# A retention, Fourier and two-layer MLP kernel: Strassen-like products summed in PSUM, normalisation moved to ScalarE, and one block's first tiles made directly

## The chip, the cores and the metric

The kernel runs on one core of one Trainium2 chip. The metric is the device time of one execution in microseconds (us); each run also has a profile of one execution, whose span is the time from the first to the last recorded instruction. Engines are named as the profile names them: PE (TensorE matmuls), PEld (its weight loads), DVE (VectorE), ACT (ScalarE), POOL (GpSimd), SP (SyncE, which issues the transfers).

## What is computed

Two sequences of 768 tokens and 512 features go through a decaying attention (8 heads of 64), a Fourier mixing over tokens and features, and then two MLP layers with a residual each. Only the MLP layers are touched by the change:

```python
def _moe_ref(x, w_ch1, w_ch2):
    X = np.fft.fft(np.fft.fft(x, axis=1), axis=2)
    u = x + np.real(X)
    un = (u - mean(u)) / np.sqrt(var(u) + 1e-06)
    return u + np.maximum(un @ w_ch1, 0.0) @ w_ch2          # 512 -> 2048 -> 512
def _moe2_ref(x, g_ln, w_ch1, w_ch2):
    xn = (x - mean(x)) / np.sqrt(var(x) + 1e-06) * g_ln
    return x + np.maximum(xn @ w_ch1, 0.0) @ w_ch2
```

The weights come as 64-bit floats. They are converted on the chip, and every operand of a matmul is a pair of float16 tensors, a high part and a low rest, so that one product is three passes (high x high, high x low, low x high).

## The kernel before, in words

**Blocks and steps.** The 1536 tokens are four blocks of 384. A layer has 16 hidden tiles of 128 features for each block, so there are 2 x 4 x 16 = 128 steps; layer one takes the blocks as 0, 1, 2, 3, layer two as 0, 1, 3, 2. Step n makes a hidden tile ("up": `mlp_up`, or `mlp_up_fast` for a pair of tiles) and applies the one of three steps earlier ("down": `mlp_down`, 9 matmuls of 512 columns into the banks `ps_y`). Everything else is put at a step number by `put` and is issued between the up and the down of that step: attention of the second sequence, weight conversion (`w_conv`), layer normalisation (`ln_tasks`), and the sums that the fast form needs. From there a scheduler that keeps the order of a priority list, but lets ready work pass, decides the order on each engine; it was not written out by hand after the first 75 us. Names carry layer, block and tile: `h1_0_7` is layer two, block 0, tile 7.

**The two forms of the up step.** The direct form (`mlp_up`, L685) is 12 matmuls of 384 columns into one PSUM bank, then ReLU on ACT (L698) and the rest on DVE (L699). The fast form (L755) makes two tiles at once from 2x2 sub-blocks in Winograd's way: seven products of six matmuls of 192 columns in place of eight. It needs sums of the weights (`w1_sums`, tiles `ws` then `sw`, four of `[128, 2, 256]` for each group g of four tiles and each kk) and sums of the normalised tokens (`un_sums`, tiles `tr`, `ts`, then `th`). The even call makes four products in two banks (`ps_1`, `ps_2`), the odd call three in two others (`ps_3`, `ps_4`). ACT and DVE put them together in SBUF (tiles `sa`, `sb`; L790 to L809), and ReLU and rest read SBUF (L779, L780). Layer two uses the fast form throughout, layer one in block 3 and from tile 4 of block 2: 46 pairs.

**The weights of layer two.** The rooms of the first weight (`w1t`) and second weight (`w2t`) are shared by the layers, so the weights of layer two can be converted only as the last block of layer one frees the rooms. `w1_unit` (16 of them, from step 52 on, one every 1.5 steps) converts a quarter of a group and after every second one calls `w1_sums` with the float32 values still at hand; the 16 of `w2` come every second step from 51.5. A conversion is three DVE operations of 512 columns (L269, L271, L273), two on ACT (L283, L284) and one on POOL (L286). In layer two the first of the four weight sums is DVE's (L722), three are POOL's (L723 to L725), and the low parts are POOL's too (L729).

**Normalisation.** `ln_a` takes mean and variance, `ln_n` (L646) subtracts and scales a row tile of 512 columns on DVE, `ln_b` splits it (ACT, POOL) and sends it through a transposing transfer.

## Time and profile before

| | before |
|---|---|
| median of 3 runs | 652.61 us (651.95 to 653.06) |
| the profiled execution | 651.21 us, of which the span is 649.0 us |
| PE, PEld busy | 585.6 us (90%), 381.1 us (59%) |
| DVE, ACT, POOL busy | 511.0 us (79%), 257.3 us (40%), 315.9 us (49%) |
| mean granted clock of TensorE | 0.972 of full speed |
| work on the chain that ended last | PE 49%, DVE 33%, issue 8% |

How to read it: shares of busy time are means over stages with different limits, so the stages are looked at one by one. Durations overlap: the next matmul starts before the one ahead is recorded as ended, and the same holds a little for DVE. The cost of a repeated matmul is therefore taken from start to start.

### The profile page before, as it was taken

The numbers are of one execution on the slowest core, as the hardware profiler recorded it, in microseconds if no ns is written. First come the engines' busy times: TensorE is split into PE (matmuls) and PEld (weight loads), VectorE is DVE, ScalarE is ACT, GpSimd is POOL, SyncE is SP. The second block draws the span as 40 slices with busy tenths as digits, with TensorE's granted clock in tenths as the row PEclk, the third lists the DMA queues.
The fourth block names the chain that finished last, engine by engine and source line by source line (L and its number), as shares of the span: only waits on it lengthen the run. The fifth ranks groups of instructions, "written<-read, shape, count | busy, mean of one in ns | idle before, by whom it ended". The sixth has DMA issues, their size and how long they took to land.

```text
span 649.0 us, 12273 instructions
## 1 busy us (share of the span) xinstructions
PE 585.6 (90%) x4733; PEld 381.1 (59%) x4733; DVE 511.0 (79%) x1040; ACT 257.3 (40%) x523; POOL 315.9 (49%) x318
## 2 busy tenths in 40 slices
PE   6958968789999999789999877987999999999997
PEld 4733734445554455466767545754676777777673
DVE  6999897999898749976599999997974754565442
ACT  3645356875532422332245553654422312221120
POOL 7865668998755564731138774787311200120000
PEclk9979899999999999999999996998999999999999
DMA  9992019885200010011044433453020014201001
GB/s 264 352 395 75 7 60 243 229 287 167 67 2 1 1 33 18 0 38 14 1 113 150 145 115 105 140 161 115 1 66 18 17 50 54 45 2 65 34 1 49
DMA packets 47141, 59.98 MB, mean 92 GB/s; under 512 B 26095, under 2 KB 31084, under 8 KB 47084
## 3 DMA queue, kind: packets, MB, share of 16 engines
q1 hardware_dynamic: 46412, 59.13, 31.2%
q8 instruction: 37, 0.61, 0.4%
q14 instruction: 20, 0.16, 0.1%
q10 hardware_dynamic: 672, 0.08, 0.1%
HBM read 50.55 MB, written 4.72 MB: 85 GB/s over the span
## 4 chain that ended last, share of the span: by engine, by line
PE 49%; DVE 33%; issue 8%; POOL 3%; ACT 3%; DMA 3%; SPq 0%; DVEq 0%; ACTq 0%; POOLq 0%
PE ps_y L820 21%; PE ps L774 17%; DVE wf L273 4%; PE ps_h L692 3%; DVE ps_w L271 3%; DVE ps_w L269 3%; DMA ws<-in_w 2%; DVE wr L717 2%; DVE h L780 2%; DVE tr L737 2%; PE ps_s L329 1%; DVE bst L627 1%; DVE h L699 1%; DVE ws L722 1%; DVE u L828 1%
## 5 line engine op out<-in xcount | busy, mean ns | idle before, releaser
L820 PE MATMUL ps_y<-w,h 128*128 128x512 f16 x1152 | 274.0, 379 | 10.5 <-DVE h L780 3.7
L820 PEld LDWEIGHTS <-h 128*128 128x128 f16 x1152 | 109.2, 98 | 119.1 <-issue 6.4
L774 PEld LDWEIGHTS <-sw 128*128 128x128 f16 x1104 | 96.8, 100 | 27.2 <-issue 9.3
L286 POOL TENSOR_TENSOR w<-wf,w 128x512 f16<-128x512 f32 x64 | 77.1, 1209 | 59.6 <-ACT w L284 59.6
L774 PE MATMUL ps<-th,sw 128*128 128x192 f16 x828 | 96.4, 252 | 7.2 <-ACT th L749 4.3
L774 PEld LDWEIGHTS <-w 128*128 128x128 f16 x828 | 72.8, 99 | 19.0 <-issue 4.9
L692 PE MATMUL ps_h<-unT,w 128*128 128x384 f16 x396 | 73.0, 326 | 10.2 <-DVE h L699 4.7
L774 PE MATMUL ps<-unT,w 128*128 128x192 f16 x552 | 63.9, 251 | 3.2 <-DVE sb L791 1.1
L692 PEld LDWEIGHTS <-w 128*128 128x128 f16 x396 | 37.3, 98 | 39.8 <-ACT w L284 6.7
L655 POOL TENSOR_TENSOR uns<-un,uns 128x512 f16<-128x512 f32 x21 | 25.3, 1206 | 70.3 <-ACT uns L654 63.8
L780 DVE SCALAR_TENSOR_TENSOR h<-sb,h 128x384 f16<-128x384 f32 x46 | 31.4, 683 | 33.7 <-ACT h L779 33.7
L750 POOL TENSOR_TENSOR th<-ts,th 128x384 f16<-128x384 f32 x28 | 27.1, 984 | 59.5 <-ACT th L749 59.5
L779 ACT ACTIVATE h<-sa 128x384 f16<-128x384 f32 x46 | 23.9, 520 | 78.3 <-DVE sa L802 75.7
L779 ACT ACTIVATE h<-sb 128x384 f16<-128x384 f32 x46 | 24.0, 521 | 70.8 <-PE ps_y L820 55.3
L729 POOL TENSOR_TENSOR sw<-ws,sw 128x512 f16<-128x512 f32 x32 | 40.7, 1281 | 20.2 <-ACT sw L728 19.9
L283 ACT ACTIVATE wf<-wf 128x512 f32<-128x512 f32 x48 | 30.0, 628 | 34.5 <-DVE wf L273 34.2
L802 DVE TENSOR_TENSOR sa<-ps,sb 128x192 f32<-128x192 f32 x46 | 16.2, 351 | 30.5 <-PE ps L774 30.2
L269 DVE TENSOR_SCALAR ps_w<-ws 128x512 int32<-128x512 int32 x54 | 36.7, 683 | 3.8 <-DMA ws<-in_w 3.7
L284 ACT CAST w<-wf 128x512 f16<-128x512 f32 x64 | 38.6, 612 | 0.8
L808 DVE TENSOR_TENSOR sb<-ps,sb 128x384 f32<-128x384 f32 x46 | 25.4, 553 | 16.7 <-PE ps L774 16.2
L271 DVE SCALAR_TENSOR_TENSOR ps_w<-ws,ps_w 128x512 int32<-128x512 int32 x54 | 36.7, 684 | 0.2
L273 DVE SCALAR_TENSOR_TENSOR wf<-ws,ps_w 128x512 int32<-128x512 int32 x54 | 36.2, 676 | 0.3
(163 smaller groups left out, 938.4 us busy)
## 6 DMA issues: line engine op xcount, KB each, us to landing
ws<-in_w SPq DMA_DIRECT2D x25, 512.0 KB, 5.8
ws<-in_w2b SPq DMA_DIRECT2D x16, 512.0 KB, 3.3
ws<-in_w1b SPq DMA_DIRECT2D x16, 512.0 KB, 3.9
kt<-in_kt SPq DMA_DIRECT2D x12, 256.0 KB, 5.0
v<-in_v SPq DMA_DIRECT2D x12, 256.0 KB, 3.9
k<-in_k SPq DMA_DIRECT2D x12, 256.0 KB, 4.4
...
```

The costliest lines, as they stand in the source:

```text
L269: dve.tensor_scalar(part, raw[:, :, 1], 3, REST, op0=ALU.logical_shift_left, op1=ALU.bitwise_and)
L271: dve.scalar_tensor_tensor(part, raw[:, :, 1], KEEP, part, op0=ALU.bitwise_and, op1=ALU.bitwise_or)
L273: dve.scalar_tensor_tensor(ti, raw[:, :, 0], 29, part, op0=ALU.logical_shift_right, op1=ALU.bitwise_or)
L283: act.activation(t, t, AF.Copy, scale=sc)
L284: act.copy(hi, t)
L286: (dve if m == 0 and i in (LD1 if kind == 1 else LD2) else pool).tensor_tensor(lo, t, hi, op=ALU.subtract)
L692: pe.matmul(ps, w[:, i, k, fo:fo + P], x[:, j, k, :], start=n == 0, stop=n == 11)
L729: pool.tensor_tensor(lo, z, hi, op=ALU.subtract)
L774: pe.matmul(ps, lhs, rhs, start=n == 0, stop=n == 5)
L779: act.activation(h[:, 0], s, AF.Relu)
L780: dve.scalar_tensor_tensor(h[:, 1], s, 0.0, h[:, 0], op0=ALU.max, op1=ALU.subtract)
L820: pe.matmul(dn[blk][j], h[:, x, j * P:(j + 1) * P], w[:, y], start=f == 0 and n == 0, stop=f == NF - 1 and n == 2)
```

## The change

**What it does.** (1) The fast form keeps its sums in PSUM. A pair has two banks, `left` and `right`, one for each half of the 384 tokens. Products that are only added to one another are accumulated by the matmuls themselves (`start` only on the first write of a bank), and DVE adds the rest in place, in PSUM. The last two products are issued as `rest()` after the step's down. ReLU and rest read PSUM, and the hidden tiles of a pair share one buffer (`h_pair`, three buffers as before, each twice as large). (2) `ln_n` becomes one tiny DVE operation and an ACT operation of 512 columns with a scale and a bias per row. (3) Block 0 of layer two makes tiles 0 to 7 directly (`F1 = 8`); its token sums come eight steps later, and the weight sums of groups 0 and 1 are made from the converted weights at steps 72 to 78 in place of 53 to 63, with two more DVE additions of 512 columns each time (L728 in the changed code, the L717 of before).

```diff
+F1 = 8
@@ ln_n
-        dve.tensor_scalar(un, u, mv[:, 0:1], rs[:, 1:2], op0=ALU.subtract, op1=ALU.mult)
+        dve.scalar_tensor_tensor(rs[:, 0:1], mv[:, 0:1], -1.0, rs[:, 1:2], op0=ALU.mult, op1=ALU.mult)
+        act.activation(un, u, AF.Identity, bias=rs[:, 0:1], scale=rs[:, 1:2])
@@ mlp_act
+            pairs[key] = up_sb.tile([P, 2, 2, TB], F16, tag="h", name=f"h{m}_{blk}_{f // 2}")
...
-        h = up_sb.tile([P, 2, TB], F16, tag="h", name=f"h{m}_{blk}_{f}")
+        h = h_pair(m, blk, f)[:, f % 2]
@@ mlp_up_fast
-                    pe.matmul(ps, lhs, rhs, start=n == 0, stop=n == 5)
+                    pe.matmul(ps, lhs, rhs, start=start and n == 0, stop=n == 5, skip_group_check=True)
...
+            left = bank("up", f"ps_1{m}_{blk}_{f}")
+            right = bank("at", f"ps_2{m}_{blk}_{f}")
+            prod(left[:, :HB], "11", "11", start=True)
+            prod(left[:, HB:TB], 2, 2)
+            prod(right[:, :HB], 1, 1, start=True)
+            act.copy(m1, left[:, :HB])
+            dve.tensor_tensor(u2, left[:, HB:TB], m1, op=ALU.add)
...
+        prod(left[:, HB:TB], 3, 3)
+        prod(left[:, :HB], "12", "21")
+        dve.tensor_tensor(u3, left[:, HB:TB], m1, op=ALU.add)
+        dve.tensor_tensor(right[:, HB:TB], right[:, :HB], u3, op=ALU.add)
+        def rest():
+            prod(left[:, HB:TB], "22", 4)
+            prod(right[:, :HB], 4, "22")
+            dve.tensor_tensor(left[:, HB:TB], left[:, HB:TB], m1, op=ALU.add)
+            dve.tensor_tensor(right[:, :HB], right[:, :HB], u2, op=ALU.add)
+            h = h_pair(m, blk, f)
+            for x, ps in enumerate((left, right)):
+                hi, lo = (h[:, :, y, x * HB:x * HB + HB] for y in range(2))
+                z = ps[:, :TB].rearrange("p (f t) -> p f t", f=2)
+                act.activation(hi, z, AF.Relu)
+                dve.scalar_tensor_tensor(lo, z, 0.0, hi, op0=ALU.max, op1=ALU.subtract)
@@ w1_unit
-        else:
+        elif 4 * g >= F1:
             w1_sums(1, g, kk, (first.pop((g, kk)), t))
@@ the plan
-    fast_from.update({(1, blk): 0 for blk in range(NB)})
+    fast_from.update({(1, blk): F1 if i == 0 else 0 for i, blk in enumerate(order[1])})
-                put(at - TL + 2 * kk, lambda m=m, blk=blk, kk=kk: un_sums(m, blk, kk))
+                put(at + f - TL + 2 * kk, lambda m=m, blk=blk, kk=kk: un_sums(m, blk, kk))
+    for g in range(F1 // 4):
+        for kk in range(2):
+            put(n0 + NF + F1 + 2 * (2 * g + kk), later(lambda g=g, kk=kk: w1_sums(1, g, kk), PR1))
...
+        if rest:
+            rest()
```

**How it moves the instructions.** The first place is DVE in the last block (layer two, block 2). Before, a pair has eight DVE operations, and all but the reads of `ps_` are on SBUF:

```order
L791 TENSOR_TENSOR sb1_2_12_7984<-ps_11_2_12_7985,sa1_2_12_7983 128x192
L795 TENSOR_TENSOR sb1_2_12_7984<-ps_21_2_12_8000,sb1_2_12_7984 128x192
L796 TENSOR_TENSOR sa1_2_12_7983<-ps_21_2_12_8000,sa1_2_12_7983 128x192
L802 TENSOR_TENSOR sa1_2_12_7983<-ps_31_2_13_8024,sb1_2_12_7984 128x192
L808 TENSOR_TENSOR sb1_2_12_7984<-ps_41_2_13_8035,sb1_2_12_7984 128x384
L780 SCALAR_TENSOR_TENSOR h1_2_12_8032<-sa1_2_12_7983,h1_2_12_8032 128x384
L809 TENSOR_TENSOR sb1_2_12_7984<-ps_41_2_13_8035,sb1_2_12_7984 128x192
L780 SCALAR_TENSOR_TENSOR h1_2_13_8050<-sb1_2_12_7984,h1_2_13_8050 128x384
```

Of the change, one period of the same engine in the same block (`ps_1` is now the left bank, `ps_2` the right one; L798 makes `u2`, L805 `u3`):

```order
L805 TENSOR_TENSOR t1_2_13_7769<-ps_11_2_12_7726,s1_2_12_7725 128x192
L806 TENSOR_TENSOR ps_21_2_12_7727<-ps_21_2_12_7727,t1_2_13_7769 128x192
L798 TENSOR_TENSOR s1_2_14_7800<-ps_11_2_14_7801,s1_2_14_7800 128x192
L811 TENSOR_TENSOR ps_11_2_12_7726<-ps_11_2_12_7726,s1_2_12_7725 128x192
L812 TENSOR_TENSOR ps_21_2_12_7727<-ps_21_2_12_7727,s1_2_12_7725 128x192
L818 SCALAR_TENSOR_TENSOR h1_2_6_7795<-ps_11_2_12_7726,h1_2_6_7795 128x2x192
L818 SCALAR_TENSOR_TENSOR h1_2_6_7795<-ps_21_2_12_7727,h1_2_6_7795 128x2x192
```

Seven operations stand where eight stood; the one of 384 columns on `sb` is gone, and the first sum of the next pair (tile 14) now stands between the sums of this one.

The second place is POOL at the end of block 0 and the start of block 1 of layer two. `sw` are low parts of weight sums, `th` of token sums; the second block's first products read `th0_1_1_0` to `th1_1_1_1`. Before:

```order
L729 TENSOR_TENSOR sw1_3_1_5746<-ws12_1_3_1_5747,sw1_3_1_5746 128x512
L286 TENSOR_TENSOR w2_1_13_5915<-wf2_1_13_5910,w2_1_13_5915 128x512
L729 TENSOR_TENSOR sw1_3_1_5746<-ws34_1_3_1_5748,sw1_3_1_5746 128x512
L750 TENSOR_TENSOR th0_1_1_0_5902<-ts12_1_1_0_5896,th0_1_1_0_5902 128x384
L750 TENSOR_TENSOR th1_1_1_0_5905<-ts34_1_1_0_5897,th1_1_1_0_5905 128x384
L750 TENSOR_TENSOR th0_1_1_1_6008<-ts12_1_1_1_6002,th0_1_1_1_6008 128x384
```

Of the change, the end of the same stretch of POOL's order:

```order
L740 TENSOR_TENSOR sw1_1_0_5646<-ws12_1_1_0_5651,sw1_1_0_5646 128x512
L740 TENSOR_TENSOR sw1_1_0_5646<-ws34_1_1_0_5652,sw1_1_0_5646 128x512
L761 TENSOR_TENSOR th0_1_1_0_5695<-ts12_1_1_0_5689,th0_1_1_0_5695 128x384
L761 TENSOR_TENSOR th1_1_1_0_5698<-ts34_1_1_0_5690,th1_1_1_0_5698 128x384
L735 TENSOR_TENSOR ws34_1_1_1_5770<-wr1_1_1_5765 128x256
L734 TENSOR_TENSOR ws12_1_1_1_5769<-ws12_1_1_1_5769,wr1_1_1_5765 128x256
L736 TENSOR_TENSOR ws34_1_1_1_5770<-wr1_1_3_5766,ws12_1_1_1_5769 128x256
L740 TENSOR_TENSOR sw1_1_1_0_5763<-ws12_1_1_1_5769,sw1_1_1_0_5763 128x512
L740 TENSOR_TENSOR sw1_1_1_1_5764<-ws34_1_1_1_5770,sw1_1_1_1_5764 128x512
L288 TENSOR_TENSOR w2_1_15_5912<-wf2_1_15_5907,w2_1_15_5912 128x512
L761 TENSOR_TENSOR th0_1_1_1_5813<-ts12_1_1_1_5807,th0_1_1_1_5813 128x384
```

The weight sums of groups 0 and 1 of layer two, which POOL made in the last block of layer one, now stand among those of group 3 and ahead of the token sums of block 1.

The third place is DVE at tile 7 of the same block 0, the last direct tile (`h1_0_3` is the buffer of tiles 6 and 7). Before:

```order
L780 SCALAR_TENSOR_TENSOR h1_0_7_5538<-sb1_0_6_5461,h1_0_7_5538 128x384
L269 TENSOR_SCALAR ps_w1_1_13_5670<-ws1_1_13_5667 128x512
L722 TENSOR_TENSOR ws12_1_3_0_5571<-wf1_1_12_5494,wf1_1_14_5561 128x256
L271 SCALAR_TENSOR_TENSOR ps_w1_1_13_5670<-ws1_1_13_5667,ps_w1_1_13_5670 128x512
L791 TENSOR_TENSOR sb1_0_8_5591<-ps_11_0_8_5592,sa1_0_8_5590 128x192
L646 TENSOR_SCALAR un1_1_1_5622<-u0_105,mv1_1_1_5543,rs1_1_1_5545 128x512
```

Of the change:

```order
L710 SCALAR_TENSOR_TENSOR h1_0_3_5264<-ps_h1_0_7_5287,h1_0_3_5264 128x384
L756 TENSOR_TENSOR ts34_1_0_1_5314<-tr1_0_3_5311,ts12_1_0_1_5313 128x192
L733 TENSOR_TENSOR ws12_1_3_0_5348<-wf1_1_12_5269,wf1_1_14_5338 128x256
L275 SCALAR_TENSOR_TENSOR wf2_1_11_5449<-ws2_1_11_5447,ps_w2_1_11_5450 128x512
L271 TENSOR_SCALAR ps_w1_1_15_5534<-ws1_1_15_5531 128x512
L798 TENSOR_TENSOR s1_0_8_5367<-ps_11_0_8_5368,s1_0_8_5367 128x192
L273 SCALAR_TENSOR_TENSOR ps_w1_1_15_5534<-ws1_1_15_5531,ps_w1_1_15_5534 128x512
L635 TENSOR_SCALAR rs1_3_1_6173<-mv1_3_1_6171 128x1
L728 TENSOR_TENSOR wr1_0_0_5399<-w1_1_0_4361 128x512
L728 TENSOR_TENSOR wr1_0_2_5400<-w1_1_0_4361 128x512
```

The first weight sum of group 3 (`ws12_1_3_0`) stands behind the rest of tile 7 in both, and the added sums of group 0 (`wr1_0_0`, `wr1_0_2`) follow it.

## Rows read from the trace of the kernel before

**Rows 1.** Busy time by stage; MLP steps from 267 us on.
```profile
core 0: us, PE busy (x) PEld busy (x) DVE busy (x) ACT busy (x) POOL busy (x), PEclk, DMA share, GB/s
182.00:267.00 85.00, 80.30 (x517) 41.35 (x516) 69.41 (x139) 26.32 (x61) 48.35 (x48) 1.00 0.05 10
...
329.00:395.00 66.00, 56.09 (x422) 37.17 (x420) 65.18 (x127) 35.37 (x67) 46.54 (x45) 0.97 0.45 135
395.00:476.00 81.00, 72.60 (x547) 50.67 (x547) 75.43 (x159) 38.50 (x77) 49.25 (x48) 0.92 0.34 101
476.00:636.00 160.00, 160.00 (x1304) 113.50 (x1303) 86.73 (x218) 36.36 (x79) 15.60 (x17) 1.00 0.16 35
```

**Rows 2.** DVE in order of time where three blocks end: start, length, instruction.
```profile
328.16 0.68 DVE L828 SCALAR_TENSOR_TENSOR u<-ps_y,u 128x512 f32<-128x512 f32 x1
...
393.99 0.68 DVE L828 SCALAR_TENSOR_TENSOR u<-ps_y,u 128x512 f32<-128x512 f32 x1
...
473.96 1.88 DVE L831 SCALAR_TENSOR_TENSOR o<-ps_y,u 128x512 f32<-128x512 f32 x3
```

**Rows 3.** PE in order of time, one pair of tiles in layer two.
```profile
502.57 0.66 PE L774 MATMUL ps<-unT,sw 128*128 128x192 f16 x6
...
504.06 2.10 PE L820 MATMUL ps_y<-w,h 128*128 128x512 f16 x9
506.00 0.66 PE L774 MATMUL ps<-unT,w 128*128 128x192 f16 x6
...
507.98 1.24 PE L820 MATMUL ps_y<-w,h 128*128 128x512 f16 x5
```

**Rows 4.** The chain that ended last: one direct tile (start, length).
```profile
163.28 1.95 PE ps_h L692 x12
```

**Rows 5.** What PE waited for, 329 to 476 us: total, times, longest.
```profile
PE ps L774 <- ACT th L749: 4.3, 3, 3.0
PE ps_y L820 <- DVE h L780: 3.7, 5, 1.3
```

**Rows 6.** Groups of DVE, 329 to 476 us: busy us, mean ns of one | idle before.
```profile
L780 DVE SCALAR_TENSOR_TENSOR h<-sb,h 128x384 f16<-128x384 f32 x16 | 14.1, 882 | 0.9 <-ACT h L779 0.9
L780 DVE SCALAR_TENSOR_TENSOR h<-sa,h 128x384 f16<-128x384 f32 x17 | 13.0, 763 | 0.0
L808 DVE TENSOR_TENSOR sb<-ps,sb 128x384 f32<-128x384 f32 x16 | 8.8, 547 | 0.2
...
L802 DVE TENSOR_TENSOR sa<-ps,sb 128x192 f32<-128x192 f32 x17 | 5.9, 345 | 0.0
...
L646 DVE TENSOR_SCALAR un<-u,mv,rs 128x512 f32<-128x512 f32 x6 | 4.6, 760 | 0.0
...
L633 DVE TENSOR_SCALAR rs<-mv 128x1 f32<-128x1 f32 x6 | 0.9, 146 | 0.0
```

**Rows 7.** Groups of the whole run, shapes apart.
```profile
L283 ACT ACTIVATE wf<-wf 128x512 f32<-128x512 f32 x48 | 30.0, 628 | 34.5 <-DVE wf L273 34.2
...
L699 DVE SCALAR_TENSOR_TENSOR h<-ps_h,h 128x384 f16<-128x384 f32 x36 | 19.6, 548 | 5.7 <-ACT h L698 5.6
...
L717 DVE TENSOR_TENSOR wr<-w 128x512 f32<-128x512 f16 x16 | 14.2, 923 | 0.0
...
L283 ACT ACTIVATE wf<-wf,gsc 128x512 f32<-128x512 f32 x16 | 11.5, 721 | 8.7 <-DVE wf L273 8.6
```

**Rows 8.** Groups of POOL, 329 to 476 us.
```profile
L286 POOL TENSOR_TENSOR w<-wf,w 128x512 f16<-128x512 f32 x32 | 38.4, 1201 | 47.2 <-ACT w L284 47.2
L729 POOL TENSOR_TENSOR sw<-ws,sw 128x512 f16<-128x512 f32 x16 | 19.1, 1196 | 0.8 <-ACT sw L728 0.5
L750 POOL TENSOR_TENSOR th<-ts,th 128x384 f16<-128x384 f32 x8 | 8.3, 1046 | 10.8 <-ACT th L749 10.8
...
L723 POOL TENSOR_TENSOR ws<-ws,wf 128x256 f32<-128x256 f32 x8 | 7.1, 881 | 1.1 <-PE ps L774 0.4 <-DMA ws<-in_w2b 0.4 <-DVE ws L722 0.4
```

**Rows 9.** PE and ACT in order of time, last pair of layer two.
```profile
631.45 0.66 PE L774 MATMUL ps<-th,sw 128*128 128x192 f16 x6
...
632.14 0.32 ACT L790 COPY sa<-ps 128x192 f32<-128x192 f32 x1 [0.42 <-PE ps L774]
```

More of the change, by code (lines that the diff above doesn't have):

```diff
@@ L694, in mlp_up, with h_pair @@
         mlp_act(m, blk, f, ps)
+    pairs = {}
+    def h_pair(m, blk, f):
+        key = m, blk, f // 2
+        if key not in pairs:
+            pairs[key] = up_sb.tile([P, 2, 2, TB], F16, tag="h", name=f"h{m}_{blk}_{f // 2}")
+        return pairs[key]
     def mlp_act(m, blk, f, ps):
-        h = up_sb.tile([P, 2, TB], F16, tag="h", name=f"h{m}_{blk}_{f}")
+        h = h_pair(m, blk, f)[:, f % 2]
         act.activation(h[:, 0], ps, AF.Relu)
@@ L757, in mlp_up_fast, with prod @@
         w, x = w1t[m, g], unT[m, blk]
-        def prod(ps, wa, xb):
+        def prod(ps, wa, xb, start=False):
             n = 0
@@ L783, in mlp_up_fast @@
-        if f % 2 == 0:
-            s = {y: f32t(f"s{y}{m}_{blk}_{f}")[:, :TB] for y in "ab"}
-            fast[m, blk] = s
-            (a1, a2), (b1, b2) = ((s[y][:, :HB], s[y][:, HB:]) for y in "ab")
-            ps = bank("up", f"ps_1{m}_{blk}_{f}")
-            prod(ps[:, :HB], "11", "11")
-            prod(ps[:, HB:TB], 2, 2)
-            act.copy(a1, ps[:, :HB])
-            dve.tensor_tensor(b1, ps[:, HB:TB], a1, op=ALU.add)
-            ps = bank("at", f"ps_2{m}_{blk}_{f}")
-            prod(ps[:, :HB], "12", "21")
-            prod(ps[:, HB:TB], 1, 1)
-            dve.tensor_tensor(b2, ps[:, HB:TB], b1, op=ALU.add)
-            dve.tensor_tensor(a1, ps[:, :HB], a1, op=ALU.add)
-            return
@@ L798, in mlp_up_fast @@
-        s = fast.pop((m, blk))
-        (a1, a2), (b1, b2) = ((s[y][:, :HB], s[y][:, HB:]) for y in "ab")
-        ps = bank("up", f"ps_3{m}_{blk}_{f}")
-        prod(ps[:, :HB], 4, "22")
-        dve.tensor_tensor(a2, ps[:, :HB], b2, op=ALU.add)
-        finish(s["a"], f - 1)
-        ps = bank("at", f"ps_4{m}_{blk}_{f}")
-        prod(ps[:, :HB], 3, 3)
-        prod(ps[:, HB:TB], "22", 4)
-        both = s["b"].rearrange("p (x t) -> p x t", x=2)
-        dve.tensor_tensor(both, ps[:, :HB].unsqueeze(1).to_broadcast([P, 2, HB]), both, op=ALU.add)
@@ L809, in mlp_up_fast @@
-        dve.tensor_tensor(b1, ps[:, HB:TB], b1, op=ALU.add)
-        finish(s["b"], f)
+        if f % 2 == 0:
+            s = f32t(f"s{m}_{blk}_{f}")
+            m1, u2 = s[:, :HB], s[:, HB:TB]
+            left = bank("up", f"ps_1{m}_{blk}_{f}")
+            right = bank("at", f"ps_2{m}_{blk}_{f}")
+            fast[m, blk] = left, right, s
+            prod(left[:, :HB], "11", "11", start=True)
[3 more added lines that the diff above has]
+            dve.tensor_tensor(u2, left[:, HB:TB], m1, op=ALU.add)
+            return None
@@ new lines, in mlp_up_fast @@
+        left, right, s = fast.pop((m, blk))
+        m1, u2 = s[:, :HB], s[:, HB:TB]
+        prod(left[:, HB:TB], 3, 3)
+        prod(left[:, :HB], "12", "21")
+        u3 = f32t(f"t{m}_{blk}_{f}")[:, :HB]
+        dve.tensor_tensor(u3, left[:, HB:TB], m1, op=ALU.add)
[11 more added lines that the diff above has]
+                dve.scalar_tensor_tensor(lo, z, 0.0, hi, op0=ALU.max, op1=ALU.subtract)
+            for y in range(2):
+                hts[m, blk, f - 1 + y] = h[:, y]
@@ L812, in tile_retention_fourier_mlp @@
+        return rest
     dn = {}
@@ L1040, in tile_retention_fourier_mlp @@
     for n in range(total + LAG):
+        rest = None
         if n < total:
@@ L1043, in tile_retention_fourier_mlp @@
             if n >= SPL:
-                (mlp_up if f < fast_from.get((m, blk), NF) else mlp_up_fast)(m, blk, f)
+                rest = (mlp_up if f < fast_from.get((m, blk), NF) else mlp_up_fast)(m, blk, f)
         for _, _, task in sorted(bg.pop(n, ()), key=lambda z: z[0]):
```

5 lines of the change are left out of this document (removed).

## The prediction, made before the changed kernel was run

> **What bounds the kernel now.** I read the busy time by stage first, then the order of time on VectorE at the ends of blocks and on TensorE inside a pair, then what TensorE waited for, then the groups of VectorE, ScalarE and GpSimd.
>
> The stages are the first thing to see [rows 1]. From 476 us on TensorE is busy all the time at full clock: nothing that only relieves another engine can help there. A pair of tiles with its two downs takes 7.35 us there, worked out from [rows 3]: 18 matmuls of 512 columns in two lots of 9 at 1.94 us each (506.00 less 504.06; 216 ns each), and 42 matmuls of 192 columns in 1.49 us (504.06 less 502.57) plus 1.98 us (507.98 less 506.00), which is 3.47 us or 82.6 ns each. So a block of eight pairs costs 58.8 us of TensorE.
>
> The two blocks before that stage are another matter. Their ends, by the last residual addition of each, are 328.8, 394.7 and 475.8 us [rows 2], so they take 65.9 and 81.2 us, 147.0 together, where TensorE needs 2 x 58.8 = 117.6. Of the 29.4 us lost, TensorE is idle for 9.9 and 8.4 (66.0 less 56.09, 81.0 less 72.60), and the rest is mostly half clock: a granted 0.97 and 0.92 of the full 2.4 GHz is 0.03 x 66 + 0.08 x 81 = 8.5 us. VectorE is busy for 65.18 of 66.0 us and 75.43 of 81.0 [rows 1]. It is the bound of these two blocks; TensorE waits for `th` and for the rests `h` [rows 5], which stand in VectorE's and ScalarE's queues.
>
> **The change, part by part.**
>
> *The fast form, VectorE.* Before, a pair is five additions of 192 columns at 0.345, one of 384 at 0.547, and rests of 0.763 and 0.882 [rows 6]: 3.92 us. After, it is five additions of 192 and two rests that read PSUM. Such rests are not in these blocks, but the direct form has them, 384 columns from PSUM in 0.548 [rows 7]. With in-place additions at the same 0.345 the pair is 2.83 us. Nothing here shows an addition with both source and target in PSUM: the lower end is the same 0.345, the upper is the 0.547 of twice the columns, which gives 3.84 us and takes back nearly all. I take 0.345, since the old additions also read PSUM once. Twelve pairs stay fast in the two blocks: 12 x 1.09 = 13.1 us off VectorE.
>
> *Direct tiles.* Four pairs of block 0 become eight direct tiles, 2 x 0.548 = 1.10 a pair in place of 3.92: 4 x 2.82 = 11.3 us off VectorE. On TensorE a direct tile is 1.95 us [rows 4], a pair 3.90 in place of 3.47: 4 x 0.43 = 1.7 us more.
>
> *Normalisation.* Six row tiles fall in these blocks: 0.760 each becomes a tiny operation of about 0.15 [rows 6], 3.7 us off VectorE. On ScalarE an operation of 512 columns costs 0.628 with constants and 0.721 with one per-row operand [rows 7]; two such operands I put at 0.814 (estimate: another 0.093). ScalarE is busy for half of these stages [rows 1], which covers the 4.9 us. The Trainium skill ("ScalarE: Activation LUTs", section "Rules for kernel authors") tells authors to multiply and add on VectorE rather than ScalarE. By that rule this move loses; as 0.15 + 0.814 less 0.760 on the path of each of 24 row tiles it would add 4.9 us to the sum. The rows agree that ScalarE is no faster, but here the other engine is the full one, so I count only the start of the program, where nothing covers it: +0.5 us.
>
> *Late weight sums.* Groups 0 and 1 need two more additions of 512 columns for each of four calls: eight of 0.923 [rows 7], 7.4 us onto VectorE.
>
> VectorE's sum over the two blocks: 65.18 + 75.43 = 140.6, less 13.1, 11.3 and 3.7, plus 7.4, is 119.9 us. TensorE needs 117.6 + 1.7 = 119.3. The two are then about equal, and the question is who comes next.
>
> *GpSimd comes next.* The weight sums of groups 0 and 1 move from block 3 of layer one into the end of block 0 of layer two, ahead of the token sums of block 1 (the second place of the order above). From the first weight sum of group 3, behind the rest of tile 7, GpSimd's queue up to the last `th1_1_1` holds 6 splits at 1.201, 12 low parts of weight sums at 1.196, 17 quarter sums at up to 0.881 and 5 low parts of token sums at 1.046 [rows 8]: 7.2 + 14.4 + 15.0 + 5.2 = 41.8 us, and about 1.5 until the first can start. TensorE's own order between the end of tile 7 and the first product on the last `th` of block 1 holds 77 matmuls of 512 columns and 188 of 192: 77 x 0.2156 + 188 x 0.0826 = 32.1 us. So TensorE waits there for 43.3 less 32.1, 11.2 us. Lower end: without the 1.5 and with the six splits let past by the waits, 2.5 us; upper end: quarter sums at 1.046, 14.0 us. I take 11.2, because GpSimd's queue is in order. Its own idle time before does not help, as it lay in other places. The idle time now costs 8.5 us of half clock for 18.3 us of idle; one gap of 11.2 would by proportion cost 5.2, one piece less than many; I take 3 (0 to 5).
>
> The two blocks: 119.3 + 11.2 + 3 = 133.5 in place of 147.0, which is **-13.5 us**.
>
> *Earlier.* From 182 to 267 us TensorE is idle for 4.7 of 85 us [rows 1] with VectorE at 69.41. The normalisation moved off VectorE, and the hidden buffers, now three of two tiles each, give room: -3 us (0 to -4.7).
>
> *The last block.* TensorE-bound, so VectorE's saving is worth nothing there. In TensorE's new order, between the second product of a pair (which `u2` needs) and the third product (which waits for `u2`) stand at least 12 matmuls of 192 and 9 of 512: 2.93 us of cover for a copy of 0.32 [rows 9] and an addition of 0.345. `u3` has about as much. No change. At the very end, though, the rest of the last pair now stands directly before its downs: an addition of 0.35, a ReLU of about 0.4 and a rest of 0.55 lie open: +1.3 us.
>
> **Sum:** -13.5 - 3 + 0.5 + 1.3 = -14.7 us. The span of 649.0 becomes 634.3, the profiled execution 651.21 becomes 636.5. The median of the runs lies 1.40 above that execution: **637.9**, said as 638.
>
> **The rivals.** A measurement of this kernel can tell about 0.2% (1.3 us) from no change.
>
> *A, as forecast*, the two blocks paced by TensorE and one late stretch of GpSimd: 638, own range 631 to 645 (GpSimd's ends, the early stage from none to all, the clock). Chance 0.52.
>
> *B, GpSimd's lateness is hidden*: its operations are shorter where VectorE is less busy, or its queue is empty when tile 7 ends. Then the two blocks take 119.3: -27.7 - 1.2 = -28.9, about 624 (621 to 627 with the clock). For it: GpSimd is busy for only half of these stages. Against it: the queue of 41.8 us. Chance 0.20.
>
> *C, the relief of VectorE is not worth time*: the in-place additions cost the upper end, or the conversions go on being paced by the chain through VectorE, ScalarE, GpSimd and the transfers. Two blocks save 2 us: -3.2, 649 (647 to 652). For it: four engines all take part in each conversion. Against it: VectorE's 98% in block 3. Chance 0.14, of which 0.03 no change.
>
> *D, slower: TensorE waits for VectorE inside each pair.* The products now accumulate into banks that VectorE and ScalarE read and write in between, so the third, fifth and later products wait for `u2`, `u3` and the addition into `right`; before, every product had a place of its own. If the cover is too short wherever VectorE's queue holds something long, each of the 42 fast pairs loses a stall. 14.7 / 42 = 0.35 us a pair is the point from which it decides; a stall of 0.5 us costs 21 us and ends at 659. A sign for it: ScalarE's copy of the first half of a bank started at 632.14, only when the product into the other half (631.45, 0.66 long) had ended [rows 9]. The Trainium skill ("PSUM — Partial Sum Buffer", section "PSUM bank collisions raise a hardware error") says that two engines may not be at the same bank at once, and that a scheduler has to order them; the trace agrees with 632.14 against 631.45. By that rule `u3` starts after the product 12x21, 6 x 82.6 ns = 0.5 us later than its data; this would leave 2.4 of the 2.93 us. Against D: the chain of 0.67 us is a quarter of the cover. Chance 0.14.
>
> That the change does not do what it says is only possible in the normalisation: were ScalarE's queue late instead, the 4.9 us come back, which lies in A's range.
>
> **Chances and range.** Faster: 0.52 + 0.20 + 0.11 = 0.83; no change 0.03; slower 0.14. From 621 to 650 lie A, B and most of C, eight in ten.
>
> **What would show it.** Right: rests from PSUM near 0.55, in-place additions near 0.35; the two blocks near 133 us; in them VectorE well below full; one wait of about 11 us for a `th` from GpSimd's queue as block 1 of layer two starts; a pair of 7.35 us in the last block. Wrong: in-place additions near 0.55 (C); no such gap (B); short waits of `ps` for VectorE in every pair, and a pair of 7.7 or more (D).

## The result and the profile after

The changed kernel takes 660.24 us (median of 4 runs, 659.63 to 663.14) against 652.28 us: a ratio of 1.013 (95% interval 1.010 to 1.0159). It is slower, where 638 us and a gain were forecast. The profiled execution took 659.63 us, its span is 657.9 us, 8.9 more than before.

The first view is the busy time of each engine over the span:

```profile
PE 587.5 (89%) x4661; PEld 375.5 (57%) x4661; DVE 479.8 (73%) x982; ACT 268.5 (41%) x543; POOL 316.2 (48%) x318
```

VectorE's work fell by 31 us (511.0 before) and the kernel got slower. So the totals say nothing, and the stages have to be set side by side. The order of time on VectorE gives the ends of the blocks, as in [rows 2] (start, length, instruction; L840 ends a block of layer one, L843 one of layer two):

```profile
185.72 0.68 DVE L840 SCALAR_TENSOR_TENSOR u<-ps_y,u 128x512 f32<-128x512 f32 x1
258.01 1.87 DVE L840 SCALAR_TENSOR_TENSOR u<-ps_y,u 128x512 f32<-128x512 f32 x3
334.77 1.88 DVE L840 SCALAR_TENSOR_TENSOR u<-ps_y,u 128x512 f32<-128x512 f32 x3
400.75 0.68 DVE L840 SCALAR_TENSOR_TENSOR u<-ps_y,u 128x512 f32<-128x512 f32 x1
479.50 1.88 DVE L843 SCALAR_TENSOR_TENSOR o<-ps_y,u 128x512 f32<-128x512 f32 x3
538.56 1.88 DVE L843 SCALAR_TENSOR_TENSOR o<-ps_y,u 128x512 f32<-128x512 f32 x3
653.41 1.34 DVE L843 SCALAR_TENSOR_TENSOR o<-ps_y,u 128x512 f32<-128x512 f32 x2 [0.39 <-PE ps_y L832]
```

The stages between these ends, start plus length, are used for every kernel below. Of the kernel before, three of the ends stand here, the others in [rows 2]:

```profile
184.06 0.67 DVE L828 SCALAR_TENSOR_TENSOR u<-ps_y,u 128x512 f32<-128x512 f32 x1
...
530.88 1.99 DVE L831 SCALAR_TENSOR_TENSOR o<-ps_y,u 128x512 f32<-128x512 f32 x3
...
643.90 1.89 DVE L831 SCALAR_TENSOR_TENSOR o<-ps_y,u 128x512 f32<-128x512 f32 x3 [4.23 <-PE ps_y L820]
```

(The first stage takes 185.6 us in experiment 11 and 189.2 in experiment 15, two kernels that differ only in their last step, so a few us there are not interpreted.)

| us | to end of block 0 | blocks 1 and 2 of layer one | next three blocks | last two blocks | rest | span |
|---|---|---|---|---|---|---|
| before | 184.7 | 144.1 | 204.0 | 112.9 | 3.2 | 649.0 |
| changed | 186.4 | 150.3 | 203.8 | 114.3 | 3.1 | 657.9 |

"Next three blocks" are block 3 of layer one and blocks 0 and 1 of layer two. The forecast of -13.5 us was for the first two of them; they take 144.7 us (336.65 to 481.38) in place of 147.0, and block 1 of layer two gives 2.0 of the 2.3 back (59.1 in place of 57.0). Blocks 1 and 2 of layer one lost 6.2 us where a gain of 3 was forecast. (The forecast spoke of 182 to 267 us, which is block 1. That block became 9.7 us shorter and block 2 15.8 us longer, so only their sum is read.)

The busy time by stage answers to [rows 1]:

```profile
core 0: us, PE busy (x) PEld busy (x) DVE busy (x) ACT busy (x) POOL busy (x), PEclk, DMA share, GB/s
186.40:336.70 150.30, 138.51 (x926) 80.92 (x925) 106.26 (x231) 46.15 (x101) 64.46 (x63) 0.95 0.07 15
336.70:401.40 64.70, 64.19 (x480) 42.29 (x479) 62.14 (x129) 39.88 (x76) 33.17 (x33) 1.00 0.59 170
401.40:481.40 80.00, 63.25 (x412) 39.67 (x410) 65.79 (x127) 34.88 (x68) 61.63 (x60) 0.89 0.24 69
...
```

In block 3 TensorE is now nearly full. In block 0 of layer two it is idle for 16.7 of 80.0 us and runs at a granted 0.89 of full speed, though neither VectorE (65.79) nor GpSimd (61.63) is full over the whole block. The chain of waits of TensorE in that block (total, times, longest) answers to [rows 5]:

```profile
PE ps L785 <- DVE s L798: 3.5, 3, 1.8
PE ps L785 <- DVE t L805: 3.1, 2, 2.6
PE ps L785 <- POOL sw L740: 2.3, 2, 1.6
PE ps_y L832 <- ACT h L817: 1.9, 1, 1.9
PE ps L785 <- DVE ps L806: 1.6, 2, 0.9
...
PE ps L785 <- ACT th L760: 1.4, 1, 1.4
...
```

No single wait of 11 us for a `th` stands there, as the forecast had it. The largest are those for `s` and `t`, which hold `u2` and `u3`: the waits within a pair that made up the slower rival. The order of time on TensorE shows two of them, at the first fast pair behind the direct tiles:

```profile
425.76 0.81 PE L832 MATMUL ps_y<-w,h 128*128 128x512 f16 x3
428.38 0.66 PE L785 MATMUL ps<-th,sw 128*128 128x192 f16 x6 [1.81 <-DVE s L798]
428.87 0.66 PE L785 MATMUL ps<-unT,w 128*128 128x192 f16 x6
432.13 1.12 PE L785 MATMUL ps<-th,w 128*128 128x192 f16 x6 [2.60 <-DVE t L805]
```

Only three matmuls of 512 columns stand ahead of the first wait and two products, twelve matmuls of 192 columns, ahead of the second; in the last block 12 matmuls of 192 and 9 of 512 give 2.93 us of cover.

In the last block that cover holds. There the order of time shows the pair as before (starts of the same lot of nine downs):

```profile
505.22 2.10 PE L832 MATMUL ps_y<-w,h 128*128 128x512 f16 x9
...
512.57 2.10 PE L832 MATMUL ps_y<-w,h 128*128 128x512 f16 x9
```

512.57 less 505.22 is 7.35 us, that of [rows 3]. At the very end an opened wait is there, 0.55 us behind a product that ends at 649.41; the last two blocks together take 1.4 us more than before.

```profile
648.75 0.66 PE L785 MATMUL ps<-unT,sw 128*128 128x192 f16 x6
649.96 4.06 PE L832 MATMUL ps_y<-w,h 128*128 128x512 f16 x18 [0.55 <-ACT h L817]
```

The groups of VectorE in the two blocks (336.7 to 481.4 us; busy, mean ns) answer to [rows 6]:

```profile
L818 DVE SCALAR_TENSOR_TENSOR h<-ps,h 128x384 f16<-128x384 f32 x24 | 12.9, 548 | 1.7 <-ACT h L817 1.7
L728 DVE TENSOR_TENSOR wr<-w 128x512 f32<-128x512 f16 x8 | 8.5, 1083 | 0.0
L748 DVE TENSOR_TENSOR tr<-unT 128x384 f32<-128x384 f16 x8 | 7.1, 926 | 0.0
L648 DVE SCALAR_TENSOR_TENSOR rs<-mv,rs 128x1 f32<-128x1 f32 x6 | 4.8, 795 | 0.1
...
L812 DVE TENSOR_TENSOR ps<-ps,s 128x192 f32<-128x192 f32 x12 | 4.3, 359 | 0.8 <-PE ps L785 0.7
...
L805 DVE TENSOR_TENSOR t<-ps,s 128x192 f32<-128x192 f32 x12 | 4.2, 349 | 7.9 <-PE ps L785 7.9
```

Rests from PSUM (0.548) and in-place additions (0.359) are as forecast. The tiny operation of the normalisation is not: 0.795 us for 128x1 elements where 0.15 was taken.

### The profile page after: what moved, and what is told of

Same layout as the page of the kernel before. It is cut to its first block, busy times and chain, and to the rows that moved or that the text cites. A ratio compares the mean times of both kernels' runs of the same rounds, so it can differ in the third digit from the quotient of the medians.

```text
span 657.9 us, 11920 instructions
## 1 busy us (share of the span) xinstructions
PE 587.5 (89%) x4661; PEld 375.5 (57%) x4661; DVE 479.8 (73%) x982; ACT 268.5 (41%) x543; POOL 316.2 (48%) x318
## 4 chain that ended last, share of the span: by engine, by line
PE 49%; DVE 28%; DMA 10%; issue 4%; POOL 3%; ACT 3%; SPq 1%; DVEq 0%; ACTq 0%; POOLq 0%
PE ps_y L832 24%; PE ps L785 20%; DVE wf L275 3%; DMA ws<-in_w 3%; DVE ps_w L271 3%; PE ps_h L695 3%; DVE ps_w L273 3%; DMA kt<-in_kt 3%; DVE wr L728 2%; DVE bst L629 2%; DVE h L710 2%; DVE tr L748 1%; DMA cdsd<-in_cd 1%; DMA pre<-in_w 1%; DMA qz<-in_qt 1%
## 5 line engine op out<-in xcount | busy, mean ns | idle before, releaser
L832 PE MATMUL ps_y<-w,h 128*128 128x512 f16 x1152 | 280.5, 382 | 5.8 <-ACT h L817 2.9
L785 PEld LDWEIGHTS <-sw 128*128 128x128 f16 x1008 | 89.0, 100 | 33.7 <-issue 17.5
L695 PE MATMUL ps_h<-unT,w 128*128 128x384 f16 x492 | 94.0, 335 | 12.8 <-DVE h L710 7.0
L785 PE MATMUL ps<-th,sw 128*128 128x192 f16 x756 | 87.2, 252 | 15.9 <-ACT th L760 8.0
L817 ACT ACTIVATE h<-ps 128x384 f16<-128x384 f32 x84 | 39.7, 489 | 75.8 <-DVE ps L811 68.0
L805 DVE TENSOR_TENSOR t<-ps,s 128x192 f32<-128x192 f32 x42 | 14.9, 354 | 56.2 <-PE ps L785 56.2
L818 DVE SCALAR_TENSOR_TENSOR h<-ps,h 128x384 f16<-128x384 f32 x84 | 44.6, 553 | 7.6 <-ACT h L817 6.2
L797 ACT COPY s<-ps 128x192 f32<-128x192 f32 x42 | 13.3, 317 | 79.7 <-PE ps L785 79.6
L637 POOL TENSOR_TENSOR rs<-rs,neghalf 128x1 f32<-128x1 f32 x24 | 14.2, 595 | 56.8 <-DVE rs L635 56.4
L739 ACT CAST sw<-ws 128x512 f16<-128x512 f32 x32 | 19.4, 615 | 46.4 <-DVE ws L734 17.6
```

What stands on the lines that cost most here:

```text
L695: pe.matmul(ps, w[:, i, k, fo:fo + P], x[:, j, k, :], start=n == 0, stop=n == 11)
L785: pe.matmul(ps, lhs, rhs, start=start and n == 0, stop=n == 5, skip_group_check=True)
L817: act.activation(hi, z, AF.Relu)
L818: dve.scalar_tensor_tensor(lo, z, 0.0, hi, op0=ALU.max, op1=ALU.subtract)
L832: pe.matmul(dn[blk][j], h[:, x, j * P:(j + 1) * P], w[:, y], start=f == 0 and n == 0, stop=f == NF - 1 and n == 2)
```

## The experiments

Three parts make eight combinations: the kernel before, the changed one and experiments 1 to 5 are seven of them (the old fast form with both other parts was not run). Ratios are to the kernel before on the same chip, with 95% intervals; stages as in the table above. A stage is read from one execution, and an edit can change the scheduler's order elsewhere too. Experiments 10, 11 and 15, the same kernel but for an edit of the last step, give 191.1, 190.1 and 189.7 us for the next three blocks, so differences of less than 1.5 us in that stage are not read.

**1. The sums in PSUM alone.** The changed kernel with `F1 = 0` and the old `ln_n`:

```diff
-F1 = 8
+F1 = 0
-        dve.scalar_tensor_tensor(rs[:, 0:1], mv[:, 0:1], -1.0, rs[:, 1:2], op0=ALU.mult, op1=ALU.mult)
-        act.activation(un, u, AF.Identity, bias=rs[:, 0:1], scale=rs[:, 1:2])
+        dve.tensor_scalar(un, u, mv[:, 0:1], rs[:, 1:2], op0=ALU.subtract, op1=ALU.mult)
```

> The kernel before with the sums in PSUM alone (normalisation on VectorE, all of layer two in the fast form). Theory W (TensorE waits for VectorE inside each pair, the slower rival of the prediction): this part alone is slower than before, by 5 us or more, with waits of ps for the new tiles s and t in every stage. Theory L (the normalisation on ScalarE is what delays layer one): this part is faster, by 3 to 10 us, most of it in the two blocks from 329 to 476 us. Theory S (the late weight sums are what eats the gain): this part is faster, by 5 to 13 us.

Measured: 648.83 us, ratio 0.9934 (0.9911 to 0.9957). The theory of waits in every pair (W) falls; this part is a gain, within the ranges of both L and S.

**2. The normalisation on ScalarE alone.** The two new lines of `ln_n` in the kernel before.

> The kernel before with the normalisation on ScalarE alone. Theory L: slower by 4 to 8 us, lost before 340 us (blocks 0 to 2 of layer one). Theories W and S: within 3 us of before, since 0.6 us of VectorE are saved for each of 24 row tiles and a step over ScalarE is added.

Measured: 653.11 us, ratio 1.0001 (0.9977 to 1.0025): nothing.

**3. Direct tiles and late weight sums alone.** `F1 = 8` with its late `put`s in the kernel before.

> The kernel before with eight direct tiles in block 0 of layer two and the late weight sums alone, in the old fast form. Theory S: slower by 3 to 10 us, lost in block 0 and at the start of block 1 of layer two, with TensorE waiting for th and sw from GpSimd. Theories W and L: faster by 2 to 6 us, since VectorE has 11.3 us less of pairs and 7.4 us more of sums there.

Measured: 658.81 us, ratio 1.0092 (1.0059 to 1.0124), by itself 0.9 of the 1.3% that the changed kernel loses. Theory S holds.

**4. No direct tiles.** The changed kernel with `F1 = 0`.

> The changed kernel with no direct tiles and the weight sums where they were (F1 = 0): the sums in PSUM and the normalisation on ScalarE stay. Theory S: faster than before by 5 to 12 us. Theory W: still slower than before, by as much as the changed kernel or more, since more pairs are in the new form. Theory L: between the two, within 4 us of before, with the loss before 340 us as in the changed kernel (6 us over blocks 1 and 2 of layer one).

Measured: 648.42 us, ratio 0.9925 (0.990 to 0.9949). It is some 5 us faster than before, at the edge of what S (5 to 12) and L (up to 4) said; both have a part. The next three blocks lose 12.7 us less than with the third part, as S said, and blocks 1 and 2 of layer one are as slow as in the changed kernel (150.8 us), as L said, so that loss has another cause.

**5. No normalisation on ScalarE.** The changed kernel with the old `ln_n`.

> The changed kernel with the normalisation back on VectorE. In layer one the last token sum of block 2 came 94.8 us after the end of block 0 before, 95.9 with the sums in PSUM alone, 96.7 with the normalisation on ScalarE alone, 99.9 with both. Theory P (the two together delay layer one): blocks 1 and 2 of layer one take about 146 us in place of 150.3, and the time is 653 to 658 us. Theory that the normalisation plays no part: 658 to 662 us, blocks 1 and 2 at 150.

Measured: 660.16 us, ratio 1.0121 (1.0092 to 1.0149). Theory P is right in its stage (144.7 us in blocks 1 and 2) and wrong in its time: the next three blocks take 207.7 us, so what layer one regains is lost there. The rival's range of time holds, its 150 us for blocks 1 and 2 do not.

| us | blocks 1 and 2 of layer one | next three blocks | last two |
|---|---|---|---|
| before | 144.1 | 204.0 | 112.9 |
| sums in PSUM (1) | 146.1 | 194.6 | 114.3 |
| normalisation (2) | 146.0 | 201.3 | 112.9 |
| direct tiles and late sums (3) | 144.1 | 210.4 | 112.9 |
| sums in PSUM and normalisation (4) | 150.8 | 191.1 | 114.3 |
| sums in PSUM and direct tiles (5) | 144.7 | 207.7 | 114.3 |
| all, the changed kernel | 150.3 | 203.8 | 114.3 |

In the next three blocks the sums in PSUM are worth -9.4 us, with the normalisation -12.9, and the direct tiles with late sums cost 6.4, 13.1 and 12.7 us (210.4 less 204.0, 207.7 less 194.6, 203.8 less 191.1). The third part eats the gain of the other two. The last two blocks lose 1.4 us wherever the sums are in PSUM, and never otherwise.

**6. The late sums early again.** The direct tiles stay; the `put`s of the late sums are removed, and `w1_unit` makes all groups:

```diff
-        elif 4 * g >= F1:
+        else:
```

> The changed kernel with the weight sums of groups 0 and 1 of layer two back where they were (made from the float32 values as the weights are converted, in block 3 of layer one); the eight direct tiles and the later token sums stay. Theory S (the late sums are what costs): 640 to 648 us, as VectorE has 7 us less and GpSimd's sums lie in the block before. Theory J (the direct tiles bring TensorE to the fast tiles of block 0 before the conversions and sums of groups 2 and 3 are ready, whatever else is there): 653 to 660 us, with block 3 of layer one as short as in the changed kernel and block 0 of layer two at 78 us or more.

Measured: 653.13 us, ratio 1.0011 (0.9988 to 1.0034), the next three blocks 195.0 us.

**7. No late sums at all.**

```diff
-                        lhs = sw[m, g, kk][(wa - 1) // 2][:, i, (wa - 1) % 2, q * P:q * P + P]
+                        lhs = sw[m, g + 2 if m and 4 * g < F1 else g, kk][(wa - 1) // 2][:, i, (wa - 1) % 2, q * P:q * P + P]
```

> The changed kernel without the late weight sums of groups 0 and 1 at all: the later blocks of layer two read those of groups 2 and 3 in their place, so tiles 0 to 7 of these blocks are computed with other weights; TensorE's work is the same. Theory S: 640 to 647 us, block 0 of layer two near 66 us. Theory J: 653 us or more, block 0 still 76 us or more, with TensorE waiting for the weight sums and conversions of groups 2 and 3.

Measured: 652.69 us, ratio 0.9995 (0.9974 to 1.0016), the next three blocks 194.9 us. So in the next three blocks the late sums cost 203.8 less 195.0, 8.8 us, and it makes no difference whether they are then made early or not at all: early, they are free. The direct tiles by themselves cost 195.0 less 191.1, 3.9 us. By the ratios of whole runs it is 1.2% (7.8 us) and 0.9% (5.6 us), each to about 0.4%; the profiled execution of experiment 6 took 650.69 us, 2.4 less than its median.

Neither theory of these two runs holds. Experiment 6 is in J's range of time and out of S's, but block 0 of layer two takes 71.2 us where J said 78 or more. Experiment 7 misses S's 640 to 647 us, and its block 0 takes 69.4 us, between S's 66 and J's 76.

What the late sums put on VectorE is seen in the busy time over the two blocks to the end of layer two's block 0, first of the changed kernel with the sums early (experiment 6), then of that without direct tiles (experiment 4):

```profile
336.50:472.40 135.90, 124.45 (x891) 80.39 (x889) 115.21 (x246) 75.28 (x143) 90.22 (x92) 0.97 0.43 122
```

```profile
339.10:472.20 133.10, 122.82 (x975) 85.12 (x973) 123.22 (x268) 75.75 (x147) 90.30 (x92) 0.99 0.47 125
```

The changed kernel has 62.14 and 65.79, 127.9 us of VectorE, 12.7 more than with the sums early, of which the eight `wr` are 8.5. TensorE's side of the same rows shows how this becomes time. It is idle for 17.3 us of the changed kernel's two blocks (144.7 less 64.19 and 63.25) and for 11.5 with the sums early, and the same matmuls (892 and 891 records) keep it busy for 127.4 and 124.5 us: in the changed kernel's block 0 the granted clock is 0.89. So of the 8.8 us some 5.8 are waits and 3.0 are matmuls at a lower clock. And the direct tiles take 8.0 us off VectorE (123.22 less 115.21) without making the two blocks shorter: 135.9 against 133.1 us.

**8. The late sums eight steps earlier.**

```diff
-            put(n0 + NF + F1 + 2 * (2 * g + kk), later(lambda g=g, kk=kk: w1_sums(1, g, kk), PR1))
+            put(n0 + NF + 2 * (2 * g + kk), later(lambda g=g, kk=kk: w1_sums(1, g, kk), PR1))
```

> The changed kernel with the late weight sums eight steps earlier (steps 64 to 70 in place of 72 to 78), beside the direct tiles. Theory Q (the loss is a collision in the second half of block 0: there the late sums stand among the conversions and sums of groups 2 and 3, and TensorE's fast tiles wait behind them): part of the 9 to 10 us comes back, 652 to 657 us. Theory V (it is the amount of work of VectorE and GpSimd in the two blocks, wherever it stands): 658 to 662 us, as the changed kernel.

Measured: 661.24 us, ratio 1.0113 (1.0086 to 1.014), the next three blocks 203.5 us. Theory V: the loss moves with them (block 3 of layer one takes 69.6 us in place of 64.8, block 0 of layer two 74.8 in place of 80.0), and the sum stays.

**9. The late groups' quarter sums on VectorE.**

```diff
-        eng = [pool if z == "p" else dve for z in SE.split("_")[m]]
+        eng = [pool if z == "p" else dve for z in ("dddd" if r_late else SE.split("_")[m])]
```

Here `r_late` is true where `w1_sums` was given no float32 values.

> The changed kernel with all four quarter sums of the late groups on VectorE, where GpSimd made three: 12 operations and about 9 us fewer on GpSimd, about 5 us more on VectorE. Theory G (GpSimd's full queue from 424 to 459 us is what TensorE waits for in the end): faster than the changed kernel by 2 to 8 us. Theory D (VectorE's queue is): slower than the changed kernel by 1 to 6 us.

Measured: 664.55 us, ratio 1.0162 (1.0132 to 1.0193). The busy time over the two blocks shows what moved:

```profile
337.20:484.70 147.50, 130.02 (x891) 82.73 (x890) 132.33 (x267) 74.73 (x143) 84.91 (x80) 0.92 0.39 112
```

GpSimd has 9.9 us less than in the changed kernel (33.17 and 61.63, 94.8), VectorE 4.4 more, and the next three blocks take 208.2 us, 4.4 more. Theory D's range holds: by the ratios it is 2.1 us slower than the changed kernel, by the times 3.3 us slower than experiment 8 on the same chip. Moving these sums from GpSimd to VectorE does not pay. That 4.4 us of work became 4.4 us of time does not show that VectorE's work counts one for one: TensorE is idle for 17.5 us of the two blocks, as in the changed kernel (17.3), it is busy for 2.6 us more with the granted clock at 0.92, and block 1 of layer two takes the other 1.7. Nor is GpSimd's queue shown to be free: the low parts of the late sums stay on it, and in the changed kernel TensorE waited 2.3 us for its `sw`.

**10. The normalisation on ScalarE in layer two alone.** As experiment 1, with

```diff
+        if m == 0:
+            dve.tensor_scalar(un, u, mv[:, 0:1], rs[:, 1:2], op0=ALU.subtract, op1=ALU.mult)
+            return
```

ahead of the two new lines of `ln_n`.

> The sums in PSUM, no direct tiles, and the normalisation on ScalarE in layer two alone. Theory P: layer one as with the sums in PSUM alone (146 us for its blocks 1 and 2), the two blocks from the end of block 2 on as with both (133 us), so 643 to 647 us, the fastest yet. Rival (the normalisation gains nothing in layer two either, the 3 us between the profiles are chance): 647 to 650 us, as with the sums in PSUM alone.

Measured: 644.92 us, ratio 0.9882 (0.9852 to 0.9912): blocks 1 and 2 of layer one at 146.3, the next three at 191.1 us. Theory P, and faster than both kernels.

**11. The last pair's late products ahead of its downs**, on experiment 10:

```diff
+        if rest and n == total - 1:
+            rest = rest()
         if n >= LAG:
             mlp_down(*step(n - LAG))
```

> The kernel with the sums in PSUM and the normalisation on ScalarE in layer two alone, with the last pair's two late products issued ahead of its step's downs. If the 1.3 us of the prediction lie open at the very end, the last block takes 54 us in place of 55.3 and the whole is 1 to 1.5 us faster than without this edit; if something else makes the last block longer, no change.

Measured: 643.67 us, ratio 0.9838 (0.9811 to 0.9866), but the last two blocks take 114.3 us as in experiment 10. The trace tells why: the last products still stand right ahead of the last 18 downs, with the same wait of 0.55 us; the edit did not change the order there, and its term stays unmeasured. The run serves as a second reading of experiment 10 on another chip, and says that such readings differ by 0.4%.

**12. The tiny operation on ScalarE**, on experiment 10:

```diff
-        dve.scalar_tensor_tensor(rs[:, 0:1], mv[:, 0:1], -1.0, rs[:, 1:2], op0=ALU.mult, op1=ALU.mult)
+        act.activation(rs[:, 0:1], mv[:, 0:1], AF.Copy, scale=-1.0)
+        act.activation(rs[:, 0:1], rs[:, 0:1], AF.Copy, scale=rs[:, 1:2])
```

> The kernel with the sums in PSUM and the normalisation on ScalarE in layer two alone, with the tiny product of mean and scale made by two tiny operations of ScalarE in place of one of VectorE. That one took 0.80 us on average in the two blocks where 0.15 was forecast. If this length costs time: 1 to 4 us faster than without this edit. If it only fills VectorE's time that TensorE does not wait for: within 1.5 us.

Measured on the same chip as experiment 11: 643.67 us, ratio 0.9845 (0.9818 to 0.9872). No difference to be told.

**13 to 15. Where the direct tiles stand.** Experiment 10 with `F1 = 8` and the weight sums early; then the same with the direct form chosen by `f >= 8` in that block; and experiment 10 again on that chip.

> The kernel with the sums in PSUM and the normalisation on ScalarE in layer two alone, plus tiles 0 to 7 of layer two's block 0 made directly, with the weight sums early as before. Theory K (after the direct tiles TensorE has no downs left to cover the waits of the first fast pairs, so what VectorE saves is lost there): 2 to 6 us slower than without the direct tiles, the two blocks at 134 to 136 us. Theory N (direct tiles are neutral or better once layer one is not delayed): within 1 us of it or faster.

> The same with tiles 8 to 15 made directly and tiles 0 to 7 in the fast form: the same number of operations on every engine, the other way round. Theory K: the fast pairs then follow fast pairs with their downs, and the wait at the turn is gone: 3 us or more faster than with tiles 0 to 7 direct. Theory A (it is the 0.43 us a pair and the amount of work, wherever the direct tiles stand): within 1.5 us of it.

> The kernel with the sums in PSUM and the normalisation on ScalarE in layer two alone once more, to stand on the same chip as these two: a ratio of 0.984 to 0.989 to the kernel before.

Measured: 647.48 us (0.9906, 0.9875 to 0.9937), 647.65 us (0.9919, 0.9891 to 0.9947) and 643.31 us (0.9838, 0.9809 to 0.9867); the next three blocks take 195.2, 194.3 and 189.7 us. The first range of theory K holds (4.2 us slower, the two blocks at 134.5), its second does not, and theory A's does: with tiles 8 to 15 direct the wait at the turn is gone, and the time is the same. The waits of TensorE from 420 to 440 us show it, first with tiles 0 to 7 direct, then with 8 to 15:

```profile
PE ps L788 <- DVE t L808: 2.4, 1, 2.4
PE ps L788 <- DVE s L801: 1.9, 1, 1.9
...
```

```profile
PE ps_y L835 <- ACT h L820: 1.9, 1, 1.9
PE ps_h L698 <- DVE h L821: 1.1, 1, 1.1
```

So the cost of the direct tiles (5.5 and 4.6 us in the next three blocks) does not hang on that one place. TensorE is idle for about as long in both, 10.8 and 10.9 us of the two blocks, though VectorE is busy for 115.2 us of them in the one and 121.1 in the other.

## Why the prediction was wrong

The forecast said a span of 634.3 us, and it is 657.9. Of the 23.6 us between them 11.2 lie in the two blocks (144.7 in place of 133.5), 9.2 in blocks 1 and 2 of layer one, 2.0 in block 1 of layer two, for which the forecast had no term, and the rest, 1.2, at the start.

**The step that failed** is the sum of the two blocks: "VectorE's sum ... is 119.9 us. TensorE needs ... 119.3. The two are then about equal", with the two blocks at 119.3 plus one late stretch. It has no term for the waits of two engines of equal work for each other. Without direct tiles and late sums the same reckoning gives 140.6 less 16 pairs x 1.09 less 3.7, 119.5 us of VectorE, and experiment 4 took 133.1, with VectorE busy for 123.2 and TensorE for 122.8: some 10 us over the busier engine. TensorE lost them in many short waits, of which these are the largest kinds of experiment 4 (total, times, longest; six kinds make 10.0 us):

```profile
PE ps L785 <- DVE s L798: 2.7, 3, 1.6
PE ps_y L832 <- DVE h L818: 2.3, 3, 1.3
PE ps L785 <- ACT th L760: 1.7, 1, 1.7
...
```

None of the six is for a converted weight, which speaks against the second half of rival C. The kernel before took only 6.4 us over VectorE's 140.6; there one engine led. So the first two parts were worth 13.9 us in these blocks (147.0 less 133.1) where the forecast's own sum has 27.5 (147.0 less 119.5).

**The third part** takes the forecast's sum from 119.5 to 133.5, a price of 14.0 us, all of it for one late stretch of GpSimd and its clock (11.2 and 3). In these two blocks it cost 11.6 (144.7 less 133.1). The two sizes are near by chance, for the stretch is not there (see below), and the sum of the rest was wrong: over the next three blocks the late sums cost 8.8 and the direct tiles 3.9. On VectorE the 7.4 was too low: the eight `wr` took 8.5 us, and VectorE has 12.7 us more in the two blocks than with the sums early. The other 4.2 are the same operations taking longer, 4.1 of it in `tr`, `ts` and the tiny operation of the normalisation. In experiment 6, over the window of its row above, two of these groups are:

```profile
L748 DVE TENSOR_TENSOR tr<-unT 128x384 f32<-128x384 f16 x8 | 5.9, 778 | 0.0
...
L648 DVE SCALAR_TENSOR_TENSOR rs<-mv,rs 128x1 f32<-128x1 f32 x6 | 3.7, 622 | 0.1
```

Where the sums stood before they were free: experiments 6 and 7 differ by whether they are made there, and take the same time. So their removal there had nothing to give. The clock was priced at 3 us; by the forecast's own reckoning the granted 0.89 of block 0 is 0.11 x 80 = 8.8 us, no less than the 8.5 before. For the direct tiles the step "11.3 us off VectorE" was right in kind (8.0 us by the two windows, against pairs that the first part had made cheaper already) and wrong in time: TensorE's 1.7 us more are there (124.45 against 122.82), and VectorE's saving does not count. Why the direct tiles cost 3.9 to 5.5 us and not 1.7 stays open; it does not depend on which eight tiles are direct.

**GpSimd.** "TensorE waits there for ... 11.2 us" at the start of block 1: not there; the longest wait for a `th` is 1.4 us. GpSimd is full for a stretch all the same, as the busy time in slices of 6 us shows (behind the length of 6.00 stands the busy time of TensorE, its weight loads, VectorE, ScalarE and GpSimd, then the granted clock):

```profile
424.00:430.00 6.00, 3.52 (x34) 2.86 (x34) 3.31 (x7) 3.35 (x7) 6.00 (x8) 1.00 0.29 100
...
448.00:454.00 6.00, 2.63 (x20) 1.49 (x18) 5.08 (x6) 1.70 (x4) 6.00 (x5) 1.00 0.11 22
454.00:460.00 6.00, 3.83 (x21) 2.86 (x21) 4.11 (x6) 1.24 (x2) 5.92 (x7) 0.52 0.01 3
```

TensorE's waits are spread over block 0 in place of one gap at its end: in the slice from 448 us it is busy for 2.63 us of 6, and in the next its clock is near the lower of its two levels (1.2 of 2.4 GHz). Which queue costs most there was not separated. The chain that ended last runs on GpSimd from 444.0 to 454.1 us and on VectorE for most of the 8 us behind, and experiment 9, with 9.9 us less on GpSimd and 4.4 more on VectorE, was no faster.

**The normalisation.** The term "0.760 each becomes a tiny operation of about 0.15" was mis-sized: 0.795 (the 0.15 is that of L633, which reads one tensor; the new operation reads two), so in these blocks the move saved VectorE nothing by itself (4.6 before, 4.8 after). It still made the next three blocks 2.7 us shorter alone and 3.5 with the sums in PSUM; experiment 12 shows that the tiny operation's length is not what TensorE waits for. Where this gain comes from stays open.

**Earlier.** "Give room: -3 us" was wrong in sign: +6.2. Blocks 1 and 2 of layer one take 144.1 us before, 146.0 with the normalisation alone and 144.7 to 147.4 with the sums in PSUM alone (experiments 1, 5 and 10 to 15, which are the same in layer one), but 150.0 to 150.8 with both (the changed kernel and experiments 4 and 6 to 9). The token sums of block 2 come late. The casts of the last of them stand here, before and after (start, length):

```profile
278.49 0.95 ACT L749 CAST th<-ts 128x384 f16<-128x384 f32 x2 [3.47 <-DVE ts L743]
```

```profile
285.33 0.95 ACT L760 CAST th<-ts 128x384 f16<-128x384 f32 x2 [2.30 <-DVE ts L754]
```

From the end of block 0 these are 94.7 and 99.9 us (ends 279.44 less 184.7, 286.28 less 186.4), and TensorE waited for them, by its waits from 259.9 to 336.7 us, 6.6 us (before, from 267.9 to 328.8 us, it did not wait for them); the granted clock of the two blocks is 0.95 where it was 1.00:

```profile
PE ps L785 <- ACT th L760: 6.6, 2, 5.3
...
```

Only with both are the two blocks at 150 us, so the combination is the cause. Which link of it delays the sums was not separated.

**What was right.** The in-place additions and the rests from PSUM (a pair is 2.86 us: two rests of 0.548 and five additions of 0.349 to 0.359), ScalarE's 0.814 us for the normalisation (median of 24), the steady pair of 7.35 us, and the 1.3 us at the end as a sum (1.4; its terms were not measured, as experiment 11 changed no order). Rival D's place was seen (waits for `u2`, `u3` and the addition into `right`: 8.2 us in block 0), not its reach: no such wait recurs in every pair, and alone the form is 0.66% faster. That its 659 us lie near the measured 660 is chance.
